# Block-sparse attention and a two-layer network: the first half in another order, and gathers spread over the period

## The chip, the cores and the metric

The kernel runs on one core of a Trainium2 chip. The metric is the device time in microseconds (us) of one execution. A kernel is run several times, and medians are given with the lowest and highest run. Most executions of one kernel agree within about 1%. Each profiled execution gives a span, which is some 1.7 to 2.0 us shorter than the time of the same run. All ledgers below are in terms of the span.

## The reference, cut to what matters

The first part is attention over 4 batches, 8 heads, 768 positions of 64 values, with positions in 24 blocks of 32. A query block sees its two neighbours, itself, the first and the last block, and three blocks drawn at random per query block (`sampled_blocks`). The first and the last query block see everything.

```python
scores = scale * np.matmul(q, k.transpose(0, 1, 3, 2))
mask = np.abs(blk_i - blk_j) <= 1                    # neighbours
mask = mask | (blk_i == 0) | (blk_j == 0) | (blk_i == 23) | (blk_j == 23)
for qb in range(24):
    for kb in sampled_blocks[qb]:                    # three drawn blocks
        mask[qb*32:(qb+1)*32, kb*32:(kb+1)*32] = True
attn = softmax(where(mask, scores, -1e9))
x = matmul(attn, v)                                  # -> (3072, 512)
h = x @ w_in                                         # (512, 2048)
out = gelu_exact(h) @ w_out                          # (2048, 512)
```

## The kernel before

The kernel goes through eight halves: 4 batches times 2 halves of 384 positions. Each half has an attention part (for four pairs of heads: scores `s`, exponentials `pt`, weighted sums `og`), transposes of the result (`psx`, copied into `xT`), a first layer (`hp`, 64 matmuls of 128x384 and 8 Gelus into `g`) and a second layer (`op`). TensorE does the matmuls, ScalarE (ACT) the exponentials and Gelus, VectorE (DVE) most copies and sums, GpSimd (POOL) the gathers, SyncE (SP) issues most DMAs. From the second half on, the second layer of one half is interleaved with the attention of the next. In the first half there is nothing to interleave.

The drawn blocks are gathered on the chip: GpSimd copies key columns (`kg`) and value rows (`v_gat`) by index. V is stored in bf16 (`v_flat`) together with three copies of itself rotated by 32, 64 and 96 partitions, so that each drawn block is also found in the partitions where the kernel uses it. DMAs from `v_flat` to `v_flat` make the rotated copies. So the gather of V depends on this chain: V lands, V is cast, three rotated copies land, three gathers per half run.

The setup and the first half, cut:

```python
st_pool = ...; p_pool = ...
first = first_ctx.enter_context(tc.tile_pool(name="first", bufs=1))   # setup tiles
...
def load_v(b):
    t = stv_pool.tile([P, NT, H, D], F32, tag="st_v", name="st_v")
    for n in range(NT):                                   # six DMAs, 256 KB each
        sp.dma_start(out=t[:, n], in_=v[b, :, n*P:n*P+P].rearrange("h p d -> p h d"))
...
pool.tensor_sub(ok, smp, qbt)           # index arithmetic of V on GpSimd, 15 operations
...
def rotate_v(b, r):
    for lo, hi, src in ((0, P - 32*r, 32*r), (P - 32*r, P, 0)):
        sp.dma_start(out=v_all[lo:hi, NT*r:NT*r+NT], in_=v_own[b % 2][src:src+hi-lo])
...
for hp in range(NPAIR):                                   # four pairs of heads
    ...  # cast and transpose q and k of this pair
    gather_k(0, 0, hp, st)
    if hp == 0:
        load_w_in(0); value_columns(); value_indices(0, dve); mark_valid(0); clear_rest()
    elif hp == 1:
        load_w_in(1)
        own_v(0, first_v, 0, dve); own_v(0, first_v, 1, act)     # casts of V
        for r in range(1, 4):
            rotate_v(0, r)
for s in range(4):
    global_v(0, s, dve)
for c in range(len(VCH)):
    gather_v(0, 0, c)
for c in range(2, 4):
    load_w_in(c)
mark_valid(1)
value_indices(1, pool)                                    # indices for odd batches
first_ctx.close()
x_pool = ctx.enter_context(tc.tile_pool(name="x_pool", bufs=2))   # takes over that memory
...
weave(attention_steps(0, 0, st), [])    # per pair: scores, then the weighted sums of the pair before
for c in range(4):
    load_w_out(c)
load_batch(1)                           # V of batch 1 on SyncE, keys and queries on GpSimd
```

`normalise` takes its scratch tile `rc` from `x_pool`. `x_pool` reuses the memory of the setup tiles.

The first layer of a half, and what is put between its steps:

```python
def step(m):                                              # eight of these
    hp_ = sc_pool.tile([P, 2, 512], F32, tag="sc", name="hp")   # two buffers
    for i in range(2):
        for ki in range(KIN):
            pe.matmul(hp_[:, i, 0:HALF], lhsT=w_in_sb[...], rhs=xT[:, ki, :], ...)
    act.activation(g[:, m:m + 2, :], hp_[:, :, 0:HALF], AF.Gelu)
...
for half in range(2 * B):
    if hb == 0:
        aux = v_steps(b, 1) + k_steps(b, 1, range(NPAIR))       # gathers for the next half
        if b > 0 and more: aux += t_steps(b + 1, (0, 1))        # q, k of the next batch
    elif b == 0: ...
    elif more:
        aux = k_steps(b + 1, 0, (0, 1)) + v_steps(b + 1, 0) + ...
    for step in spread(hidden_steps(b, hb, sts[b]), aux): step()
    ...
    weave(attention_steps(next half), output_steps(this half))
```

The softmax here doesn't subtract the row's maximum and nothing guards it: scores larger than these inputs give would overflow.

Of the kernel before, what the change touches and what calls it, by code (L numbers as in the profile page):

```python
# [10 lines left out]
F32 = mybir.dt.float32  # L11
# [68 lines left out]
def kernel(  # L80
# [24 lines left out]
    p_pool = ctx.enter_context(tc.tile_pool(name="p_pool", bufs=2))  # L105
    first_ctx = ExitStack()
# [15 lines left out]
    def load_v(b):  # L122

        t = stv_pool.tile([P, NT, H, D], F32, tag="st_v", name="st_v")
        for n in range(NT):
            sp.dma_start(out=t[:, n], in_=v[b, :, n * P:n * P + P].rearrange("h p d -> p h d"))
        return t
# [10 lines left out]
    src = dataclasses.replace(sampled_blocks.tensor, shape=[NB, NR * 2], dtype=I32)  # L138
    sp.dma_start(out=raw, in_=bass.AP(tensor=src, offset=0, ap=[[0, P], [1, NB * NR * 2]]))

    first_st = {}
    for hp in range(NPAIR):
        first_st["k", hp] = load_first("k", hp, sp)
        first_st["q", hp] = load_first("q", hp, sp)
        if hp == 1:
            first_v = load_v(0)

    def iota(out, pattern, base, mult):
# [10 lines left out]
                       pattern=[[-1, P]], channel_multiplier=1)  # L159
    lane = msk.tile([P, 1], F32, name="lane")  # L160
# [26 lines left out]

    sbi = msk.tile([P, NB, NR], I32, name="sbi")
# [26 lines left out]
    part8 = msk.tile([P, 2], I32, name="part8")  # L215
    dve.tensor_single_scalar(part8[:, 0:1], part_i, 7, op=ALU.bitwise_and)
    dve.tensor_single_scalar(part8[:, 1:2], part_i, 8, op=ALU.bitwise_and)
    lane8 = msk.tile([P, 2], F32, name="lane8")
    dve.tensor_copy(lane8, part8)
    pool.tensor_scalar(lane8[:, 0:1], lane8[:, 0:1], float(GW), None, op0=ALU.mult)  # L220
    pool.tensor_scalar(lane8[:, 1:2], lane8[:, 1:2], 0.125, None, op0=ALU.mult)
    slotm = msk.tile([P, NR], F32, name="slotm")
    for s in range(NR):
        pool.tensor_scalar(slotm[:, s:s + 1], slot, float(s), None, op0=ALU.is_equal)

# [3 lines left out]
    dve.tensor_tensor(turn, smp_i, slot_i.unsqueeze(2).to_broadcast([P, NQ, NR]), op=ALU.subtract)  # L229
    dve.tensor_single_scalar(turn, turn, 3, op=ALU.bitwise_and)  # L230
    colf = msk.tile([P, NQ, NR], F32, name="colf")
    dve.tensor_copy(colf, turn)
    dve.tensor_single_scalar(turn, smp_i, 2, op=ALU.arith_shift_right)
    rowf = msk.tile([P, NQ, NR], F32, name="rowf")
    dve.tensor_copy(rowf, turn)
    dve.scalar_tensor_tensor(colf, colf, 6.0, rowf, op0=ALU.mult, op1=ALU.add)
    dve.tensor_scalar(colf, colf, -float(NULL), None, op0=ALU.add)


    ok = msk.tile([P, NQ, NR], F32, name="ok")  # L240
    pool.tensor_sub(ok, smp, qbt)
    pool.tensor_mul(ok, ok, ok)
    pool.tensor_scalar(ok, ok, 3.5, None, op0=ALU.is_gt)
    glob = msk.tile([P, NQ, NR], F32, name="glob")
    pool.tensor_scalar(glob, smp, -1.0, float(NB - 1), op0=ALU.mult, op1=ALU.add)
    pool.tensor_mul(glob, glob, smp)
    pool.tensor_scalar(glob, glob, 0.5, None, op0=ALU.is_gt)
    pool.tensor_mul(ok, ok, glob)
    differ = msk.tile([P, NR, NQ], F32, name="differ")
    pairs = ((1, 0), (2, 0), (2, 1))  # L250
    for n, (a, c) in enumerate(pairs):
        pool.tensor_sub(differ[:, n], smp[:, :, a], smp[:, :, c])
    pool.tensor_mul(differ, differ, differ)
    pool.tensor_scalar(differ, differ, 0.5, None, op0=ALU.is_gt)
    for n, (a, c) in enumerate(pairs):
        pool.tensor_mul(ok[:, :, a], ok[:, :, a], differ[:, n])

    def value_columns():
        dve.tensor_mul(colf, colf, ok)
        for s in range(NR):  # L260
            dve.scalar_tensor_tensor(
                base_v, colf[:, :, s], slotm[:, s:s + 1], base_v, op0=ALU.mult, op1=ALU.add)
        dve.tensor_scalar(valid, base_v, float(NULL) - 0.5, None, op0=ALU.is_lt)
# [20 lines left out]

    mask_x = const.tile([P, NT, P], BF16, name="mask_x")
    kgl = [[const.tile([P, P], BF16, name=f"kgl{i}{hp}") for hp in range(NPAIR)] for i in range(2)]
    qgl = [const.tile([P, P], BF16, name=f"qgl{hp}") for hp in range(NPAIR)]
    vgl = [const.tile([P, NPAIR, 2 * VW], BF16, name=f"vgl{i}") for i in range(2)]
    n_all = (NAT1 + NT) * H * GW
    v_flat = const.tile([P, 2 * -(-n_all // DW) * DW], BF16, name="v_flat")  # L290
    v_all = v_flat[:, 0:2 * n_all].rearrange("p (n h e) -> p n h e", h=H, e=2 * GW)
    v_gat = [const.tile([P, NQH, H, 2 * GW], BF16, name=f"v_gat{i}") for i in range(2)]
    v_own = [v_all[:, 0:NT], v_all[:, NAT1:NAT1 + NT]]
    for t in kgl[0] + qgl:
        dve.memset(t, 0.0)

    def clear_rest():
        dve.memset(v_flat[:, 2 * NULL * H * GW:], 0.0)
        for i in range(2):
            dve.memset(v_own[i][:, :, :, D:2 * GW], 1.0)  # L300
# [6 lines left out]
        for i in range(2):  # L307
            dve.memset(vgl[i], 0.0)
            for h in range(2):
                dve.memset(vgl[i][64 * h:64 * h + 64, :, h * VW + D:h * VW + D + 1], 1.0)  # L310
        for t in kgl[1]:
            dve.memset(t, 0.0)
# [11 lines left out]
    def load_w_in(c):  # L324
        pool.dma_start(out=w_in_sb[:, :, 512 * c:512 * c + 512],
                            in_=w_in_v[:, :, 512 * c:512 * c + 512])

    def load_w_out(c):
        pool.dma_start(out=w_out_sb[:, 4 * c:4 * c + 4, :], in_=w_out_v[:, 4 * c:4 * c + 4, :])
# [3 lines left out]
    def own_v(b, st_v, i, eng):  # L333
        n = slice(3 * i, 3 * i + 3)
        cast(eng, v_own[b % 2][:, n, :, 0:D], st_v[:, n])

    def rotate_v(b, r):

        for lo, hi, src in ((0, P - 32 * r, 32 * r), (P - 32 * r, P, 0)):
            sp.dma_start(out=v_all[lo:hi, NT * r:NT * r + NT],  # L340
# [11 lines left out]
    def gather_v(b, hb, c):  # L352
# [3 lines left out]
            v_flat.bitcast(F32).rearrange("p (n e) -> p n e", e=DW),  # L356
# [20 lines left out]
    def gather_k(b, hb, hp, st):  # L377
        kg = kg_pool.tile([P, NQH, P], BF16, tag="kg", name="kg")
# [7 lines left out]
    def scores(b, hb, hp, st):  # L386
# [3 lines left out]
        pt = p_pool.tile([P, 2, 2, 512], BF16, tag="pt", name="pt")  # L390
# [165 lines left out]
    sts = [dict() for _ in range(B)]  # L556
    st = sts[0]
    first_bf = {}
    for hp in range(NPAIR):
        for w in "kq":  # L560
            t = first.tile([P, 2, NT * D], BF16, name=f"bf_{w}{hp}")
            act.copy(t, first_st[w, hp])
            transpose_qk(0, hp, w, t, dve if w == "k" else act, st)
            globals_qk(0, hp, w, dve, st)
        gather_k(0, 0, hp, st)
        if hp == 0:
            load_w_in(0)
            value_columns()
            value_indices(0, dve)
            mark_valid(0)  # L570
            clear_rest()
        elif hp == 1:
            load_w_in(1)
            own_v(0, first_v, 0, dve)
            own_v(0, first_v, 1, act)
            for r in range(1, 4):
# [123 lines left out]
```

## Time and profile before

The three runs before the prediction gave a median of 349.69 us (347.67 to 350.56). The profiled execution took 350.82 us, a little above that range, and has a span of 349.0 us.

| what | before |
|---|---|
| V cast, rotated copies issued | 27.2 us |
| first gather of V starts, last one ends | 47.4, 55.5 us |
| first matmul of the first layer (first hp) | 74.9 us |
| first-layer stage of the first half, first hp to next scores | 11.6 us |
| first hp of batch 1 | 148.9 us |
| span | 349.0 us |

The table of stretches of the kernel before gives, for each stretch of time, its length, the busy time of each engine with the number of instructions, the granted TensorE clock as a share of full speed, the DMA share and GB/s.

```profile
core 0: us, PE busy (x) PEld busy (x) DVE busy (x) ACT busy (x) POOL busy (x), PEclk, DMA share, GB/s
0.00:75.00 75.00, 25.12 (x409) 19.76 (x410) 34.05 (x125) 22.71 (x30) 32.88 (x68) 1.00 0.87 176
75.00:149.00 74.00, 64.49 (x883) 39.34 (x893) 29.22 (x61) 37.26 (x49) 25.94 (x34) 0.98 0.58 114
149.00:349.00 200.00, 175.92 (x2243) 106.25 (x2267) 71.34 (x147) 94.86 (x126) 56.62 (x69) 0.99 0.27 67
```

In the first 75 us TensorE is busy a third of the time, and no other engine is busy for half of it. The prediction reads such a stretch as a chain of dependencies. The DMA share of 0.87 leaves a rival reading, that the stretch is limited by the bytes it moves. After the stretch, TensorE is busy for 88% of the time.

The timeline of the kernel before shows that chain. The columns are start, duration, engine, operation, what it writes and reads, and in brackets the idle time of the engine ahead of it with what ended it. SPq and ACTq lines are issues of DMAs by a sequencer, not the transfers.

```profile
3.16 9.57 SPq L54 DMA_DIRECT2D st_v<-in_v_dram  x6
...
26.07 1.04 DVE L54 CAST v_flat<-st_v 128x1536 bf16<-128x1536 f32 x1
27.19 6.47 SPq L54 DMA_DIRECT2D v_flat<-v_flat  x6
33.70 14.23 SPq L54 DMA_DIRECT2D st_v<-in_v_dram  x6
...
47.41 1.66 POOL L54 INDIRECT_COPY v_gat_222<-v_flat,idx_v_163 128x1024 f32 x1 [10.47 <-DMA st_v<-in_v_dram]
51.06 1.66 POOL L54 INDIRECT_COPY v_gat_222<-v_flat,idx_v_163 128x1024 f32 x1 [2.00 <-issue]
54.03 1.45 POOL L54 INDIRECT_COPY v_gat_222<-v_flat,idx_v_163 128x768 f32 x1 [1.31 <-issue]
...
60.92 0.17 DVE L54 RECIPROCAL rc<-od 128x2 f32<-128x2 f32 x1 [17.54 <-POOL idx_v_164 L54]
...
74.14 0.73 DVE L54 COPY xT<-xdT 128x128 bf16<-128x128 bf16 x1
74.93 2.76 PE L54 MATMUL hp<-xT,w_in_sb 128*128 128x384 bf16 x16 [1.27 <-DVE xT L54]
78.63 7.96 PE L54 MATMUL hp<-xT,w_in_sb 128*128 128x384 bf16 x48 [0.94 <-ACT g L54]
86.52 0.34 PE L54 MATMUL s_983<-tq,tk 64*128 64x128 bf16 x6
```

The reader is to see four things. The cast of V ends at 27, and the copies are issued at once. The first gather names a load of V as its releaser, but it reads `v_flat`; the loads of the next V were issued in the same stretch, and the profile names the event that came last. The first two gathers start 3.65 us apart although each is busy for 1.66. VectorE waits 17.5 us, to 60.9, for GpSimd's last write of an index tile that `rc` has nothing to do with: this is the reuse of memory.

How much of that wait reaches TensorE is told by TensorE's own list of waits, here of the first 75 us of the kernel before (total, number of times, longest):

```profile
PE og L54 <- POOL v_gat_222 L54: 11.6, 3, 5.6
...
PE od L54 <- DVE xd L54: 3.0, 1, 3.0
```

TensorE lost 3.0 us behind the tile that VectorE's wait delayed, not 17.5. Most of VectorE's wait lay beside TensorE's own waits for the gathers. The same list from 149 us on, the steady part, holds these:

```profile
PE psx L54 <- DVE xT L54: 4.7, 5, 1.9
...
PE ps L54 <- DVE tk L54: 1.6, 2, 0.8
...
PE ps L54 <- DVE tq L54: 0.7, 2, 0.3
```

### The profile page before, as it was taken

The numbers are of one execution on the slowest core, as the hardware profiler recorded it, in microseconds if no ns is written. First come the engines' busy times: TensorE is split into PE (matmuls) and PEld (weight loads), VectorE is DVE, ScalarE is ACT, GpSimd is POOL, SyncE is SP. The second block draws the span as 40 slices with busy tenths as digits, with TensorE's granted clock in tenths as the row PEclk, the third lists the DMA queues.
The fourth block names the chain that finished last, engine by engine and source line by source line (L and its number), as shares of the span: only waits on it lengthen the run. The fifth ranks groups of instructions, "written<-read, shape, count | busy, mean of one in ns | idle before, by whom it ended". The sixth has DMA issues, their size and how long they took to land. (4 is left out here: it accounts for less than half of the span.)

```text
span 349.0 us, 8094 instructions
## 1 busy us (share of the span) xinstructions
PE 265.5 (76%) x3532; PEld 165.3 (47%) x3568; DVE 134.6 (39%) x333; ACT 154.8 (44%) x205; POOL 115.4 (33%) x171
## 2 busy tenths in 40 slices
PE   1216103779889878897879989888989898989995
PEld 1115002655555545454545565454645564555552
DVE  6785200530454614714641438233634343025101
ACT  3427103326653365344633576146524771664420
POOL 3603137744101455434313545332215453200000
PEclk9999999999999989999998999999999999999999
DMA  6967975995099401910297349000750001001001
GB/s 215 240 156 164 206 152 78 187 201 81 2 251 234 69 2 34 198 43 2 68 254 160 73 67 178 32 2 2 211 162 2 3 32 62 2 27 37 30 31 61
DMA packets 43252, 34.98 MB, mean 100 GB/s; under 512 B 26192, under 2 KB 38608, under 8 KB 43216
## 3 DMA queue, kind: packets, MB, share of 16 engines
q1 hardware_dynamic: 32656, 25.54, 29.0%
q0 software_dynamic: 10560, 8.91, 16.8%
q8 instruction: 28, 0.46, 0.5%
q14 instruction: 8, 0.07, 0.1%
HBM read 27.34 MB, written 6.29 MB: 96 GB/s over the span
## 5 line engine op out<-in xcount | busy, mean ns | idle before, releaser
L54 PE MATMUL op<-w_out_sb,g 128*128 128x512 bf16 x348 | 88.7, 387 | 4.6 <-issue 4.0
L54 ACT ACTIVATE g<-hp 128x768 bf16<-128x768 f32 x64 | 51.8, 811 | 89.9 <-PE hp L54 89.9
L54 PE MATMUL hp<-xT,w_in_sb 128*128 128x384 bf16 x512 | 86.8, 327 | 2.2 <-DVE xT L54 1.3
L54 POOL INDIRECT_COPY kg<-tk,idx_k 128x704 f32 x32 | 40.6, 1268 | 81.1 <-issue 44.4
L54 PEld LDWEIGHTS <-w_in_sb 128*128 128x128 bf16 x512 | 49.5, 98 | 36.4 <-issue 3.4
L54 DVE TENSOR_TENSOR pt<-pt,mask_x 128x768 bf16<-128x768 bf16 x32 | 22.9, 718 | 90.3 <-ACT pt L54 90.3
L54 PEld LDWEIGHTS <-g 128*128 128x128 bf16 x384 | 34.5, 99 | 33.6 <-issue 2.2
L54 PEld LDWEIGHTS <-pt 128*32 128x32 bf16 (+1 forms) x992 | 24.1, 100 | 23.4 <-issue 19.9
L54 DVE COPY tk<-ps 128x768 bf16<-128x768 bf16 x16 | 15.2, 947 | 40.5 <-PE ps L54 40.5
L54 ACT ACT_TABLE_LOAD x16 | 20.5, 1283 | 15.4 <-PE hp L54 7.0
L54 ACT ACTIVATE pd<-sd 128x768 bf16<-128x768 f32 x16 | 13.0, 813 | 31.0 <-PE sd L54 30.8
L54 DVE COPY os<-op 128x512 f32<-128x512 f32 x24 | 16.5, 686 | 23.4 <-PE op L54 23.4
L54 POOL INDIRECT_COPY v_gat_222<-v_flat,idx_v_164 128x1024 f32 (+1 forms) x6 | 9.5, 1587 | 41.6 <-DMA st_v<-in_v_dram 20.6
L54 PEld LDWEIGHTS <-tk 64*128 64x128 bf16 (+1 forms) x288 | 13.8, 102 | 20.1 <-issue 17.4
L54 PEld LDWEIGHTS <-kg 64*128 64x128 bf16 x704 | 13.2, 94 | 13.1 <-issue 8.8
L54 POOL INDIRECT_COPY v_gat_222<-v_flat,idx_v_163 128x1024 f32 (+1 forms) x6 | 9.5, 1586 | 28.4 <-issue 17.9
L54 DVE TENSOR_TENSOR x<-og,rc 128x384 bf16<-128x384 f32 x32 | 17.8, 557 | 1.1
L54 PE MATMUL psx<-ident,x 128*128 128x128 bf16 x96 | 9.8, 226 | 8.7 <-DVE xT L54 5.8
L54 PE MATMUL og<-v_gat_222,pt 128*32 128x65 bf16 x352 | 6.8, 207 | 11.6 <-POOL v_gat_222 L54 11.6
L54 PEld LDWEIGHTS <-x 128*128 128x128 bf16 x96 | 7.0, 101 | 14.2 <-issue 9.2
L54 POOL INDIRECT_COPY v_gat_223<-v_flat,idx_v_163 128x1024 f32 (+1 forms) x6 | 9.5, 1575 | 11.5 <-issue 9.2
L54 DVE COPY xT<-psx 128x512 bf16<-128x512 bf16 (+1 forms) x24 | 9.6, 402 | 9.4 <-PE psx L54 9.2
(360 smaller groups left out, 321.2 us busy)
## 6 DMA issues: line engine op xcount, KB each, us to landing
st_v<-in_v_dram SPq DMA_DIRECT2D x24, 256.0 KB, 5.1
out_dram<-os SPq DMA_DIRECT2D x24, 256.0 KB, 2.6
v_flat<-v_flat SPq DMA_DIRECT2D x8, 594.0 KB, 6.1
v_flat<-v_flat SPq DMA_DIRECT2D x8, 396.0 KB, 6.7
st<-in_k_dram POOLq DMA_DIRECT2D x6, 384.0 KB, 8.8
st<-in_q_dram POOLq DMA_DIRECT2D x6, 384.0 KB, 10.2
w_in_sb<-in_moe_w_in_dram POOLq DMA_DIRECT2D x4, 512.0 KB, 7.6
w_out_sb<-in_moe_w_out_dram POOLq DMA_DIRECT2D x4, 512.0 KB, 9.2
```

The costliest lines, as they stand in the source:

```text
L54: return self._tc.keep_in_program_order(f(*args, **kwargs))
```

## The change

The intent is to shorten the chain of the first half and to spread GpSimd's work. V is loaded ahead of the other pairs and cast tile by tile, and the rotated copies are issued right after. The index arithmetic moves from GpSimd to VectorE. The scores of all four pairs run while the copies and gathers of V are under way, and the four weighted sums follow together. `x_pool` is allocated first, so its tiles reuse no setup memory. Keys and queries of the later three pairs are loaded by GpSimd straight into bf16, which saves six of ScalarE's eight casts (0.83 us each). The weights come in four DMAs of 1 MB where there were eight of 512 KB. V of batch 1 is issued from ScalarE's queue inside the first Gelu stage. From the second half on, gathers move out of the Gelu stages into the attention parts too, and one VectorE step copies four pieces where four separate steps did.

The diff, cut to its core:

```diff
+    x_pool = ctx.enter_context(tc.tile_pool(name="x_pool", bufs=2))
     first_ctx = ExitStack()
-    def load_v(b):
+    def load_v(b, eng):
...
-            sp.dma_start(out=t[:, n], in_=v[b, :, ...])
+            eng.dma_start(out=t[:, n], in_=v[b, :, ...])
...                              # ok, differ, glob: 15 pool operations removed
     def value_columns():
-        dve.tensor_mul(colf, colf, ok)
+        dve.tensor_sub(ok, smp, qbt)
+        dve.tensor_mul(ok, ok, ok)
+        ...                      # 14 more, all on VectorE, then base_v as before
...
     def load_w_in(c):
-        pool.dma_start(out=w_in_sb[:, :, 512*c:512*c+512], ...)
+        f = slice(1024 * c, 1024 * c + 1024)
+        pool.dma_start(out=w_in_sb[:, :, f], in_=w_in_v[:, :, f])
...
+    first_pair(0); clear_mask(); clear_globals(0, dve); first_pair(1)
+    for n in range(NT):
+        own_v(0, first_v, n, n + 1, (dve, act)[n % 2])
+    for r in (2, 1, 3):
+        rotate_v(0, r, sp)
+    value_columns(); value_indices(0, dve)
+    scores(0, 0, 0, st); dense_scores(0, st)
+    for c in range(2):
+        load_w_in(c)
+    first_pair(2); scores(0, 0, 1, st); first_pair(3)
+    ...                          # scores of pairs 2 and 3, gather_v, global_v
+    value_indices(1, dve)
+    for c in range(2):
+        load_w_out(c)
+    dense_weighted(0, 3, st); transpose_xd(st)
+    for hp in range(NPAIR):
+        weighted(0, 0, hp, st)
+    for m in range(MH):
+        transpose_x(0, 0, m, st)
+    place_xd(0, 0, st)           # the last copy into xT
-    weave(attention_steps(0, 0, st), [])
...
-        if hb == 0:
-            aux = v_steps(b, 1) + k_steps(b, 1, range(NPAIR))
...
+        for n, step in enumerate(spread(hidden_steps(b, hb, sts[b]), aux)):
+            step()
+            if half == 0 and n == 0:
+                sts[1]["st", "v"] = load_v(1, act)
+        if half == 0:
+            load_batch(1)
...
+            after[0] = own_steps(b + 1)
+            if b > 0:
+                after[3] = k_steps(b + 1, 1, (0,))
+                after[4] = k_steps(b + 1, 1, (1,))
+                after[len(main) - 4] = v_steps(b + 1, 0)
```

## The prediction

> **What bounds the kernel now.** In the table of stretches TensorE is busy 25.1 of the first 75.0 us and 240.4 of the remaining 274 (88%). TensorE's timeline has the first hidden-layer matmul (hp) at 74.93 us; afterwards its waits sum to roughly 28 us, half of it short turns that must stay. So the first 75 us are a dependency chain, the rest is TensorE.
>
> **The chain of the first 75 us (timelines, waits).** V has landed at 16.5 us, but VectorE, held by a wait for GpSimd's index arithmetic, the indices and 6.5 us of memsets, casts its half only at 26.1; the rotated copies of V are issued from 27.2 and in place at about 45. The three gathers of V end at 55.5 (3.65 us each with their gaps). VectorE waits 17.5 us, to 60.9, for GpSimd's last index write: the normalisation's scratch reuses the memory of the setup tiles. Only then do the remaining pairs run.
>
> **What changes.** V is cast tile by tile as it lands; rotated copies start near 17 us, beside the first weights. From the traffic of before (copies, one weight chunk and the next V took about 18 us together) I estimate that the copies, sharing with 4.2 MB of weights, are in place near 38. Index arithmetic moves to VectorE (some 30 operations of 0.2 to 0.4 us, 8.4 us), after the copies' issue. Scores of all four pairs fit in before 38. Gathers of V: 38 + 3 x 3.65 = 49. Then four weighted sums and the transposes, about 7 us: first hp at 56.5 instead of 74.9. Gain 18.4 us. The reuse wait vanishes: that scratch is now allocated earlier.
>
> **What it costs.** V of batch 1 is issued from ScalarE's queue, after the first of eight Gelus. Six such issues took 5.6 us on SyncE with little beside them, 9.6 and 14.2 in traffic (SyncE's timeline), holding the sequencer. [...] this trace says about 1 us each. hp has two buffers, so TensorE stalls in the first hidden stage: I estimate 7 us (5 to 11). The second-layer weights, issued near 50, land before that stage ends.
>
> **Later.** GpSimd starts earlier in each stage: waits for kg (3.7 us in batch 1's first half), for xT behind a VectorE copy of rotated V (about 2.5 us), and doubled transposes waiting for VectorE (2.3 us) should mostly go: minus 5 us. Larger weight DMAs save nothing by themselves.
>
> 349.7 - 18.4 + 7 - 5 = 333; I predict **332 us**, 80% range **321 to 343**. Faster by over 2%: 0.91; within 2%: 0.07; slower: 0.02.
>
> **What would show it.** First hp near 56 us (52 to 61); rotated copies issued near 17; v_gat done near 49; no VectorE wait on an index tile. In the first hidden stage a gap of 5 to 11 us between first and second Gelu, filled by DMA issues, and a TensorE wait for g nearly as long; that stage's end near 75 instead of 86.5. TensorE busy within 5 us. Later stages equal or up to 3 us shorter per batch.
>
> **What would make it wrong.** If issues on ScalarE don't hold it, the end is near 325. If the weights slow the rotated copies further, or VectorE's index arithmetic delays the later pairs' keys so that the gathers of V start late, first hp comes at 62 or later and the gain shrinks to 12 us. If batch 1's keys and queries, now loaded after the first hidden stage, arrive late, TensorE stalls near 95 us.

349.7 - 18.4 + 7 - 5 came to 333, and the 7 us are an estimate from the issue times of 5.6 to 14.2 us in the trace of before.

## The result, and the profile after

The changed kernel took 333.77 us (median of 4 runs, 333.33 to 336.02) against 349.74 us (347.67 to 350.56, 4 runs). The ratio is 0.9565, with a 95% interval of 0.9505 to 0.9625. Here and below, a ratio is the mean time of one kernel's fast runs over the mean time of the other's in the same rounds, so it is not quite the ratio of the medians that are quoted.

The profiled spans are 349.0 and 332.2 us. They differ by 16.8 us and the medians by 16.0, since the profiled run of before was slower than its median. The ledger, read from TensorE's timelines:

| | before | after | difference | predicted |
|---|---|---|---|---|
| rotated copies issued | 27.2 | 21.5 | | near 17 |
| first gather of V starts | 47.4 | 43.5 | | 38 |
| last gather of V ends | 55.5 | 51.6 | | 49 |
| first hp | 74.9 | 60.6 | -14.3 | 56.5 (-18.4) |
| first-layer stage of the first half | 11.6 | 18.5 | +6.9 | +7 |
| from there to the end | 262.5 | 253.1 | -9.4 | -5 |
| span | 349.0 | 332.2 | -16.8 | -16.4 |

The stretches of the changed kernel, cut at the first hp, at the end of that stage and at the first hp of batch 1:

```profile
0.00:60.60 60.60, 23.70 (x408) 18.98 (x409) 36.89 (x142) 18.35 (x26) 23.01 (x37) 0.98 0.84 155
60.60:79.10 18.50, 14.64 (x65) 7.36 (x65) 0.46 (x6) 6.84 (x8) 9.05 (x9) 0.79 0.76 137
79.10:139.20 60.10, 52.60 (x819) 32.65 (x829) 29.05 (x61) 30.29 (x41) 20.25 (x30) 1.00 0.73 142
139.20:332.20 193.00, 173.67 (x2243) 105.38 (x2267) 69.78 (x147) 94.81 (x126) 55.50 (x69) 1.00 0.28 69
```

TensorE's work in the first half is nearly the same, 23.7 us against 25.1; the stretch became shorter because less of it is waiting. The second stretch has a granted clock of 0.79 where the others have about 1.

The timeline of the changed kernel, with the lines that answer to those of before:

```profile
2.22 15.07 SPq L54 DMA_DIRECT2D st_v<-in_v_dram  x6
20.85 0.62 ACT L54 CAST v_flat<-st_v 128x512 bf16<-128x512 f32 x1 [1.49 <-DMA st_v<-in_v_dram]
21.49 5.37 SPq L54 DMA_DIRECT2D v_flat<-v_flat  x6
43.51 1.66 POOL L54 INDIRECT_COPY v_gat<-v_flat,idx_v 128x1024 f32 x1 [7.36 <-issue]
50.12 1.44 POOL L54 INDIRECT_COPY v_gat<-v_flat,idx_v 128x768 f32 x1 [1.30 <-issue]
...
57.77 2.79 DVE L54 COPY xT<-xdT 128x128 bf16<-128x128 bf16 x1
58.86 1.64 POOL L54 INDIRECT_COPY v_gat<-v_flat,idx_v 128x1024 f32 x1 [2.01 <-issue]
60.61 6.40 PE L54 MATMUL hp<-xT,w_in_sb 128*128 128x384 bf16 x24 [3.22 <-DVE vgl L54]
63.54 3.21 ACTq L54 DMA_DIRECT2D st_v<-in_v_dram  x3
64.69 0.81 ACT L54 ACTIVATE g<-hp 128x768 bf16<-128x768 f32 x1
66.79 3.13 ACTq L54 DMA_DIRECT2D st_v<-in_v_dram  x3
69.97 1.51 ACT L54 ACTIVATE g<-hp 128x768 bf16<-128x768 f32 x2 [4.47 <-issue]
70.83 8.34 PE L54 MATMUL hp<-xT,w_in_sb 128*128 128x384 bf16 x40 [3.82 <-ACT g L54]
79.10 0.34 PE L54 MATMUL s<-tq,tk 64*128 64x128 bf16 x6
```

Three readings follow. First, SyncE's sequencer needed 15.07 us to issue the six loads of the first V, where before it needed 9.57. Other loads of keys and queries ran at the same time. The last tile of V was cast at 21.5, not at 17. That the slow issue is the reason is not shown: in e5 below the issue took 10.85 us, and the last cast still ended at 21.6. Second, the last VectorE copy into `xT` took 2.79 us. It took 0.73 before, and such a copy is a matter of 0.3 us (it took 0.18 to 0.44 in the seven later halves of the changed kernel, and ScalarE did the same copy in 0.30 us in an experiment below). Third, ScalarE issued the six loads of V between its first Gelus. The gap between the first and the second is 4.47 us, the stretch of issues is filled, and TensorE waited 3.82 us for `g`.

The matmuls of that stage also took longer each. The 24 ones from 60.61 took 6.40 us, 0.27 us each; before, the 48 ones from 78.63 took 7.96 us, 0.17 us each. The records of the granted clock, read in stretches of 2 us, give 0.50 from 60.6 to 65.0, 1.00 to 70.8, a mean of 0.73 to 73, 0.50 to 75, and nearly 1 from there. TensorE idled 3.22 us ahead of the first hp and 3.82 us inside the stage, and its matmuls then ran at the recorded 0.50 for 4.4 us and for about 3.4 us (worked out from the means). Read in stretches of 0.5 us, the clock is at 0.50 from 58.5 on, about 1 us after TensorE had gone idle, and again from 72.0 on, about 1 us after its work had resumed. What makes the clock fall and come back is not shown: in e1 below, TensorE idled 4.70 us ahead of the first hp, and the record gives 1.00 from 57.0 to 70.0.

So the +6.9 us of this stage consist of about 2.9 us more waiting (3.82 against 0.94) and 4.0 us of slower matmuls (14.74 us of `hp` against 10.72).

TensorE's waits from the first hp of batch 1 to the end of the changed kernel, those answering to the three lines shown of before:

```profile
PE psx L54 <- DVE xT L54: 2.4, 5, 0.5
```

The waits for `xT` fell from 4.7 to 2.4 us, and those for `tk` and `tq` (2.3 us) are gone from the list. In the part between, waits for `kg` fell from 3.7 to 1.2 us. These are the later gains.

### The profile page after: what moved, and what is told of

It is laid out like the page before. It is cut to its first block, busy times and chain, and to the rows that moved or that the text cites. A ratio compares the mean times of both kernels' runs of the same rounds, so it can differ in the third digit from the quotient of the medians.

```text
span 332.2 us, 8067 instructions
## 1 busy us (share of the span) xinstructions
PE 264.6 (80%) x3532; PEld 164.4 (49%) x3568; DVE 136.2 (41%) x356; ACT 150.3 (45%) x201; POOL 107.8 (32%) x144
## 3 DMA queue, kind: packets, MB, share of 16 engines
q0 software_dynamic: 11072, 10.09, 20.1%
## 5 line engine op out<-in xcount | busy, mean ns | idle before, releaser
L54 PE MATMUL hp<-xT,w_in_sb 128*128 128x384 bf16 x512 | 90.7, 336 | 7.1 <-ACT g L54 3.8
L54 PE MATMUL op<-w_out_sb,g 128*128 128x512 bf16 x348 | 86.2, 379 | 4.4 <-issue 3.8
L54 ACT ACTIVATE pt<-s 128x1024 bf16<-128x1024 f32 (+2 forms) x96 | 58.9, 687 | 27.2 <-issue 11.6
L54 POOL INDIRECT_COPY kg<-tk,idx_k 128x704 f32 x32 | 39.3, 1229 | 84.4 <-issue 66.8
L54 POOL INDIRECT_COPY v_gat<-v_flat,idx_v 128x1024 f32 (+1 forms) x24 | 38.2, 1591 | 79.2 <-issue 44.4
L54 DVE TENSOR_TENSOR pt<-pt,mask_x 128x768 bf16<-128x768 bf16 x32 | 20.1, 630 | 103.8 <-ACT pt L54 103.6
L54 ACT ACT_TABLE_LOAD x16 | 20.5, 1283 | 30.7 <-PE hp L54 24.1
L54 DVE COPY tk<-ps 128x768 bf16<-128x768 bf16 x16 | 15.3, 956 | 27.3 <-PE ps L54 27.2
L54 DVE COPY os<-op 128x512 f32<-128x512 f32 x24 | 16.5, 687 | 23.7 <-PE op L54 23.7
L54 PE MATMUL ps<-ident,st 128*64 128x128 bf16 x384 | 16.7, 244 | 11.7 <-ACT st L54 9.2
L54 PEld LDWEIGHTS <-st 128*64 128x64 bf16 x384 | 13.5, 124 | 16.4 <-ACT st L54 9.4
L54 PE MATMUL s<-tq,kg 64*128 64x32 bf16 x704 | 14.2, 175 | 8.6 <-ACT g L54 4.4
L54 PE MATMUL sd<-qgl,tk 128*128 128x128 bf16 x96 | 9.2, 240 | 13.6 <-ACT pt L54 13.6
L54 PE MATMUL og<-v_gat,pt 128*32 128x65 bf16 x704 | 12.4, 199 | 7.0 <-POOL v_gat L54 7.0
## 6 DMA issues: line engine op xcount, KB each, us to landing
w_in_sb<-in_moe_w_in_dram POOLq DMA_DIRECT2D x2, 1024.0 KB, 20.6
```

The costliest lines, as they stand in the source:

```text
L54: return self._tc.keep_in_program_order(f(*args, **kwargs))
```

## The experiments

The theory after the result, which the experiments then had to test: the total came from the order of the first half and the order of the loop. The order gave 14 us, of which a few were lost to VectorE being held beside the gathers, and half was given back to issues of V on ScalarE. The rivals: the gain came from the vanished reuse wait (17.5 us in VectorE's list), from larger weight DMAs, or from taking the index arithmetic off GpSimd. All experiments change the kernel after, except one that changes the kernel before. Every result was correct. The runs were made on three chips; each was compared with the kernel before on its own chip, whose medians there were 350.82 (group of e1 to e4), 351.17 (e5 to e8) and 351.77 us (e9 to e12).

| run | median (range, runs) us | ratio to before (95%) | first hp | stage | first hp of batch 1 | span |
|---|---|---|---|---|---|---|
| before | 349.74 (347.67-350.56, 4) | 1 | 74.9 | 11.6 | 148.9 | 349.0 |
| after | 333.77 (333.33-336.02, 4) | 0.9565 (0.9505-0.9625) | 60.6 | 18.5 | 139.2 | 332.2 |
| e1 | 333.08 (329.1-334.76, 6) | 0.9464 (0.9401-0.9527) | 61.3 | 12.8 | 138.2 | 331.0 |
| e2 | 333.91 (331.84-335.59, 6) | 0.9521 (0.9469-0.9573) | 58.3 | 12.8 | 136.8 | 331.0 |
| e3 | 333.86 (331.88-335.64, 6) | 0.9506 (0.9453-0.956) | 56.2 | 21.8 | 138.0 | 332.2 |
| e4 | 339.22 (337.48-339.63, 4) | 0.965 (0.9589-0.9711) | 67.2 | 17.5 | 144.7 | 337.8 |
| e5 | 332.74 (331.51-335.8, 6) | 0.946 (0.9418-0.9501) | 60.0 | 19.7 | 139.8 | 334.0 |
| e6 | 332.02 (331.31-332.59, 4) | 0.945 (0.9408-0.9492) | 60.2 | 15.8 | 136.0 | 330.8 |
| e7 | 341.77 (340.82-342.03, 4) | 0.9725 (0.9683-0.9768) | 59.7 | 19.6 | 142.1 | 340.0 |
| e8 | 325.54 (324.13-326.99, 6) | 0.9269 (0.9233-0.9305) | 57.9 | 12.8 | 130.0 | 324.4 |
| e9 | 348.41 (345.01-350.41, 4) | 0.9946 (0.9879-1.0012) | 71.4 | 12.2 | 145.8 | 343.2 |
| e10 | 335.47 (334.68-336.09, 4) | 0.955 (0.9491-0.961) | 58.5 | 20.1 | 139.1 | 334.1 |
| e11 | 336.88 (336.63-338.36, 4) | 0.9608 (0.9545-0.967) | 60.2 | 20.7 | 141.0 | 335.3 |
| e12 | 322.31 (321.33-327.16, 6) | 0.9171 (0.9122-0.922) | 54.2 | 13.0 | 127.7 | 322.0 |

One run each of e1 (334.76), e9 (350.41) and e12 (327.16) fell in the slow state; they are in the medians and ranges but not in the ratios. All profiled runs are fast ones. The first hp of the kernels e5, e7 and e10, whose first half is that of after or nearly so, scatters between 58.5 and 60.6. Their first-layer stage scatters as well (18.5 to 20.1 us, with after). Differences of 2 us in those columns are not worth an explanation unless the timeline shows their cause.

One caution holds for every comparison with after. It was not run again beside the experiments, and medians and ratios disagree about them. By medians e1, e2, e3, e5 and e6 lie within 1.8 us of after. By ratios (their difference times 351 us) they lie 3.5, 1.5, 2.1, 3.7 and 4.0 us below it, and only the intervals of e5 and e6 are clear of after's. So whether these five gained such amounts in total is not settled; what follows rests on the timelines.

### e4: the old order inside the new first half

```diff
-    scores(0, 0, 0, st); dense_scores(0, st)
     for c in range(2): load_w_in(c)
-    first_pair(2); scores(0, 0, 1, st); first_pair(3)
-    ...                                   # scores of all pairs, then weighted sums
+    first_pair(2); first_pair(3); mark_valid(0)
+    for c in range(len(VCH)): gather_v(0, 0, c)
+    for s in range(4): global_v(0, s, dve)
+    value_indices(1, dve)
+    for c in range(2): load_w_out(c)
+    weave(attention_steps(0, 0, st), [])  # pair by pair, as before
```

> The changed kernel, with only the order of the first half put back: scores and weighted sums of the pairs alternate as in the kernel before, so the weighted sum of pair 0 stands in TensorE's queue before the scores of pairs 2 and 3. Theory: after the last gather of V (51.6 us) three pairs of scores must still be done; the kernel before took 19.4 us from its last gather to first hp, the changed kernel 9.0. Expect first hp at 68 to 71 instead of 60.6, total 342 (340 to 345). Rival: the gain comes from V being ready earlier and the order hardly matters: total within 3 us of 333.8.

Measured: 339.22 us, first hp at 67.2, which is 6.6 us later than after although its gathers ended 2.4 us earlier (49.2). By medians and by spans the order is worth 5.5 us, by the ratios 3 us (0.965 against 0.9565, in intervals that overlap). So the direction stands, and the order by itself is worth less than the expected 8 us. From the end of its last gather to the first hp e4 took 18.0 us; before took 19.5 and after 9.0. One line of e4's timeline shows one reason why the old order is dear beside the gathers:

```profile
53.21 4.43 DVE L54 TENSOR_TENSOR pt<-pt,mask_x 128x768 bf16<-128x768 bf16 x1 [2.73 <-ACT pt L54]
```

The multiplication by the mask takes 0.56 us elsewhere. It fell among the gathers for the next half and took 4.43 us. In the new order these multiplications are done before the gathers start.

### e9: the kernel before, with the reuse wait taken away

```diff
 for s in range(4):
     global_v(0, s, dve)
+value_indices(1, pool)
 for c in range(len(VCH)):
     gather_v(0, 0, c)
 ...
 mark_valid(1)
-value_indices(1, pool)
```

The wait is not removed by hand; the index tile is only finished before the gathers.

> The kernel before, with one line moved: the second index computation of GpSimd stands ahead of its gathers of V instead of behind them, where GpSimd is idle anyway. Theory: the wait of 17.5 us that VectorE showed for that index (to 60.9 us) overlaps with the wait for the gathers, which end at 55.5, so only some 4 us of it were on the path. Expect no VectorE wait on an index tile, first hp at 70 to 72.5 instead of 74.9, total 346 to 348 against 350 to 351 for the kernel before. Rival: the wait was the bottleneck of the first half, as its length suggests; then first hp comes 10 us or more earlier and the total is under 341.

Measured: 348.41 us, ratio 0.9946 (0.9879 to 1.0012), so the total is not clearly different. The first hp came at 71.4, 3.5 us earlier, and that of batch 1 3.1 us earlier. (The profiled run was the fastest of e9, so its span of 343.2 flatters it.) VectorE's reciprocal now waits 12.29 us, for TensorE. Of the 3.5 us, 1.4 came from gathers that ran earlier in this run (the last ended at 54.0, not 55.5). From there to the first hp e9 took 17.4 us, against 19.5 before, although its last copy into `xT` took 1.76 us beside a gather (0.73 before). So the wait of 17.5 us was worth some 2 to 3 us, in keeping with the 3.0 us that TensorE's own list showed. The rival "the reuse wait made the gain" falls.

### e10: small weight DMAs

```diff
-        f = slice(1024 * c, 1024 * c + 1024)
+        f = slice(512 * c, 512 * c + 512)
...
-    for c in range(2):
+    for c in range(4):
         load_w_in(c)
```

The second-layer weights were split in the same way.

> The changed kernel, with both weights loaded in four DMAs each as in the kernel before instead of two. Theory: larger weight DMAs save nothing by themselves; GpSimd needs 1.5 us more to issue each weight, and the transfers are limited by the shared DMA engines. Expect total within 1.5 us of the changed kernel's 333.8, weights landing at the same time within 2 us. Rival: the larger rows make the transfers faster, so smaller ones slow the rotated copies and the first gather comes 2 us later or more: total 336 or more.

Measured: 335.47 us, ratio 0.955 (0.9491 to 0.961) against 0.9565. The median is 1.7 us above after's, just outside the expected 1.5; the ratio is not above it, and the first gather of V came at 42.6 (43.5 in after), so not later. GpSimd needed 3.04 us to issue the four first-layer DMAs (1.56 for two in after), and they landed 19.4 us after their issue (20.6 in after, medians). The DMA engines were busy meanwhile (share 1.02 from 21.5 to 43.5 us in after). No effect of the size of the weight DMAs is seen, as the prediction said.

### e11: the index arithmetic back on GpSimd

```diff
+    pool.tensor_sub(ok, smp, qbt)
+    pool.tensor_mul(ok, ok, ok)
+    ...                          # the 15 operations of before
     def value_columns():
-        dve.tensor_sub(ok, smp, qbt)
-        ...                      # nine VectorE operations
```

> The changed kernel, with the index arithmetic (which sampled blocks count) put back on GpSimd, at the place it had before. Theory: its place matters only because in the kernel before it stood between VectorE and the cast of V; here V is cast first, so GpSimd's 5 us of small operations only delay the loads of keys and queries of heads 4 to 7 (to 12 us) and the first key gather (to 17 us), and the rotated copies still end at 41. Expect first gather of V at 40.5 to 43.5 us, total within 2 us of 333.8. Rival: the arithmetic on GpSimd holds the chain again, first gather at 45 or later, total 336 or more.

Measured: 336.88 us, ratio 0.9608 (0.9545 to 0.967), which overlaps with after's interval. Both expectations were missed: the first gather of V came at 44.8 (40.5 to 43.5 expected), and the median is 3.1 us above after's (2 expected), past the 336 that the rival named. VectorE finished the first indices at 24.1 instead of 26.8, since it had fewer of the operations; the first gather of V began 1.3 us later than in after, and the first hp came at the same time; and ScalarE's V issues happened to take 1.7 us longer, which lengthened the stage to 20.7 us. By medians the engine of the arithmetic is worth 3.1 us, by ratios 1.5 us, and these runs do not separate that from zero. So this rival is not shown to give any of the gain.

### e7: the old loop after the new first half

The loop from the second half on was put back, with `load_v` on SyncE in its old place; the first half stayed.

```diff
-        elif hb == 0 and more:
-            for hp in (0, 1):
-                aux += t_steps(b + 1, (hp,)) + k_steps(b + 1, 0, (hp,))
-        ...
-        after[0] = v_steps(nb_, 1) + k_steps(nb_, 1, range(2 * (b > 0), NPAIR))
+        elif hb == 0:
+            aux = v_steps(b, 1) + k_steps(b, 1, range(NPAIR))
+            if b > 0 and more: aux += t_steps(b + 1, (0, 1))
+        ...
```

> The changed kernel's first half, but the order of gathers, casts and copies of V from the second half on as in the kernel before. From the first hp of batch 1 to the end the kernel before took 200.1 us, the changed kernel 193.0. Theory: these 7 us are the spread gathers and the casts moved off VectorE's busy stretches, not the early start. Expect this stretch to take 199 to 201 us again, total 340 (338 to 342). Rival: the stretch was longer in the kernel before through its later start or its clock; then it stays near 193 and the total near 334.

Measured: 341.77 us, span 340.0, which is 7.8 us more than after. From the first hp of batch 1 to the end it took 197.9 us, against 193.0 after and 200.1 before; 199 to 201 were expected. TensorE's waits over that stretch of e7 hold these lines:

```profile
PE psx L54 <- DVE xT L54: 4.9, 5, 1.9
...
PE ps L54 <- DVE tk L54: 1.6, 2, 0.8
...
PE ps L54 <- DVE tq L54: 0.7, 2, 0.3
```

They are the waits of before, to within 0.2 us. They explain 4.8 of the 4.9 us. The other 2.9 us lie before batch 1, where waits for `kg` rose from 1.2 to 3.3 us and those for `xT` from 1.0 to 2.0 (3.1 us together). The loop's order is thus worth 7.8 us by the spans, 8.0 by the medians and 5.6 by the ratios, whose intervals are apart. The 2.2 us between 197.9 and 200.1 have no wait to explain them. They lie within the scatter of the profiles: the stretch took 197.4, 197.9 and 200.1 us in the three kernels with the old loop (e9, e7, before) and 192.8 to 195.0 us in the eleven others. The means differ by 4.4 us, about as much as the waits.

### e1: V of batch 1 on SyncE, behind the first gather

```diff
-            if half == 0 and n == 0:
-                sts[1]["st", "v"] = load_v(1, act)
...
+    fence = const.tile([P, 2], BF16, name="fence")
+    sp.dma_start(out=fence, in_=v_gat[0][:, 0, 0, 0:2])   # waits for the first gather
+    sts[1]["st", "v"] = load_v(1, sp)
```

> The changed kernel, with V of batch 1 issued from SyncE instead of ScalarE; a tiny copy that reads the first gathered V holds it back until then, so that it loads in the stretch (46 to 52 us) in which the DMA engines are idle. Theory: the six issues hold ScalarE between its first and second Gelu (4.5 us gap, TensorE waits 3.8 us for g). Expect: no DMA issue on ScalarE, gap between these Gelus under 1 us, TensorE wait for g about 1 us, total 3 us less (330.5, 329 to 332). Rival: the first hidden stage is long because the clock is lowered there (0.66) and because weights still load; then the total stays at 333 to 334 and the stage's length (18.5 us) hardly changes.

Measured: the first-layer stage fell from 18.5 to 12.8 us, so the issues on ScalarE cost 5.7 us there, clock included. The issues on SyncE took 5.3 us. But the median is 333.08, hardly below 333.77 (by the ratio the gain is 3.5 us, in intervals that overlap), and the first hp of batch 1 came only 1.1 us earlier. Two things took the gain. TensorE waited 4.7 us for `kg` ahead of batch 1 (1.2 in after), since the rotated copies of batch 1 and its gathers of V kept their places in the program (e8 moves both): the gathers of V began at 100.4 us (101.5 in after), and the key gathers came behind them. And the last copy was held still longer, as the timeline of e1 shows:

```profile
56.95 4.27 DVE L54 COPY xT<-xdT 128x128 bf16<-128x128 bf16 x1
57.54 1.64 POOL L54 INDIRECT_COPY v_gat<-v_flat,idx_v 128x1024 f32 x1 [2.01 <-issue]
61.21 1.65 POOL L54 INDIRECT_COPY v_gat<-v_flat,idx_v 128x1024 f32 x1 [2.02 <-issue]
61.28 12.90 PE L54 MATMUL hp<-xT,w_in_sb 128*128 128x384 bf16 x64 [4.70 <-DVE vgl L54]
```

The copy ended at 61.22, just when the next gather began. In after it ended at 60.56, with the end of a gather at 60.50; in e2 and e6, where it took 2.29 and 2.11 us, it ended within 0.1 us of the end of a gather as well. So VectorE was held: these copies lasted until a gather was over, or until the next one started. What decides which of the two goes first is not shown: each of the four copies began in the 2 us ahead of a gather in which GpSimd records no work (in after at 57.77, with gathers that ended at 56.84 and began at 58.86). Nor is the end a rule: the multiplication of e4 ended at 57.64, 1.2 us into a gather. Not every operation was held: `x<-og,rc`, which reads what TensorE wrote, kept its 0.56 us beside a gather (after, at 55.71). That its length, 2.1 to 4.3 us, depends on where among the gathers the copy happens to fall is my reading of four such cases. The stage's 12.8 us are still 1.2 more than before: the matmuls of its start took 0.30 us each (9 in 2.70 us), the pace that goes with a clock of 0.50 in after (8 in 2.39 us from 60.6), with no ScalarE issue in sight (the record of the clock says 1.00 there). The stages of e2, e8 and e12, also without these issues, took 12.8 to 13.0 us. What slows this part is not shown; in e4, with the old order, the first 16 matmuls took 4.38 us too (2.76 in before).

### e2: V of batch 1 on SyncE, without the fence

```diff
-                sts[1]["st", "v"] = load_v(1, act)
+                sts[1]["st", "v"] = load_v(1, sp)
```

> The changed kernel, with V of batch 1 issued from SyncE right behind the rotated copies (about 27 us), nothing holding it back. Theory of issue cost: ScalarE's gap goes as in e1. Theory of contention: 1.6 MB more in the queue while rotated copies and first weights load; the rotated copies, ahead in the same queue, keep their time (first gather still at about 43.5 us, within 1.5), the first weights land by 50, before they are needed: total as e1, 330.5. Rival: the early V takes DMA time from the rotated copies, the first gather comes at 46 or later, and the total is 333 or more.

Measured: 333.91 us, so the expected 330.5 was missed. SyncE issued the loads from 28.1 to 47.4, 19.3 us for six, right in the traffic of the rotated copies and the weights. The first gather of V was not delayed (41.2). The first hp of the second half came 6.8 us earlier than in after, that of batch 1 only 2.5 us: TensorE waited 5.2 us for `kg`. As in e1, the local gain was taken by the same later wait.

e2 also bears on the rival that bytes limit the first half. Ahead of the first hp, before moved about 13.2 MB, after 9.4 and e2 11.0 (estimates, from GB/s times length). e2 moved 1.6 MB more than after, and its first hp came 2.4 us earlier, so these bytes did not set it. What the other traffic is worth that after moved out of the first half was not tested.

### e3: the last copy on ScalarE

```diff
-        dve.tensor_copy(st["xT", hb][:, :, c], st["xdT"][...])
+        cast(eng, st["xT", hb][:, :, c], st["xdT"][...])     # eng = act for half 0
```

> The changed kernel, with the last copy before the first hidden stage (xT from xdT, 128x128, 2.79 us on VectorE) put on ScalarE, which is idle there. Theory: VectorE's copy is held for the length of GpSimd's running gather, which a copy on ScalarE would not be. Expect the copy at 0.2 to 0.4 us, first hp 2 to 2.5 us earlier (58 to 58.7), total 331.5 (330 to 333). Rival: the copy waits for something else that takes until 60.5, such as its input or the weights; then first hp stays at 60.6 and the total at 333.8.

Measured: 333.86 us, no gain in the median (2.1 us by the ratio, in intervals that overlap), but what the edit did is plain in the timeline of e3:

```profile
45.23 0.30 ACT L54 COPY xT<-xdT 128x128 bf16<-128x128 bf16 x1 [6.11 <-DVE xdT L54]
...
56.18 5.85 PE L54 MATMUL hp<-xT,w_in_sb 128*128 128x384 bf16 x24 [0.61 <-DVE xT L54]
59.87 8.16 ACTq L54 DMA_DIRECT2D st_v<-in_v_dram  x4
68.94 9.06 PE L54 MATMUL hp<-xT,w_in_sb 128*128 128x384 bf16 x40 [6.91 <-ACT g L54]
```

The copy took 0.30 us, beside a gather (45.10 to 46.75), and the first hp came at 56.2 instead of 60.6. Of these 4.4 us, 2.1 came from gathers that began earlier in this run (41.45), and the remaining 2.3 are the hold that vanished. That the hold is as long as the gather, as the theory had it, is not what after shows: its copy took 2.79 us and the gather 1.64. Then ScalarE's issues of V took 8.16 us for four (3.13 for the last three in after); that the loads of the second-layer weights, issued from 49.4, slowed them is a guess, not shown. TensorE waited 6.91 us for `g`, and the stage ended at 77.9, 1.2 us earlier than after. A gain ahead of a stage of DMA issues was given back in it.

### e5: keys and queries of the later pairs loaded after the first pair

```diff
     new_x(0, 0, st)
+    first_pair(0)
     for w in "kq":
         st["st", w, 1] = load_qk(0, w, 1)
-    first_pair(0)
```

> The changed kernel, with the loads of keys and queries of heads 4 to 7 issued on GpSimd after its first key gather (about 12 us) instead of at 6.9. Theory: V lands 4 us later than in the kernel before (last cast ends 21.5 instead of 17 to 18) because these 1.6 MB of loads take DMA time from it. Expect the last cast of V to end at 18 to 19.5, rotated copies issued from there, first gather of V at 39 to 41 instead of 41.1 to 43.5, and almost no gain in the end of the first hidden stage, as the V of batch 1 on ScalarE sets that: total 333 (331 to 335). Rival: V lands late because SyncE issues slowly on its own account; then the last cast still ends at 21 or later.

Measured: the last cast of V still ended at 21.6 us. SyncE's issue became shorter (10.85 us), but the moved loads, issued at about 12.5, ran beside the last tiles of V. The first gather came at 42.9 (43.5 in after). The rival, that SyncE issues slowly on its own account, does not fit either: the issue was 4.2 us shorter, and the cast ended no earlier. This is a miss: the edit did not give V the free way that it was meant to give, so what an earlier V would be worth stays open.

### e6: first-layer weights after the key gathers

```diff
     scores(0, 0, 0, st); dense_scores(0, st)
-    for c in range(2): load_w_in(c)
     first_pair(2); scores(0, 0, 1, st); first_pair(3)
+    for c in range(2): load_w_in(c)
```

> The changed kernel, with the first weights issued on GpSimd only after the key gathers of all four pairs (about 35.6 us instead of 21.7). Theory: the rotated copies took 20 us because the weights share the DMA engines; alone they should take about 10 us from 21.5 and be in place at 32 to 33, so GpSimd's own queue sets the first gather of V: 39.5 to 40.5 us. The weights then land near 51, before first hp at 57 to 58.5. Total 333 (331 to 335), as in e3. Rival: the rotated copies are slow by themselves and first gather stays at 41 to 43.5.

Measured: 332.02 us. The rotated copies landed in 5 to 8 us where they needed 7 to 14 in after (medians of the three pairs, from issue to landing), and the first gather of V came at 39.3, 4.2 us earlier than in after. So the weights did hold the copies, and the copies the weights: these landed in 10.2 us instead of 20.6. But the first hp moved by only 0.5 us. The timeline of e6 shows the new obstacle:

```profile
41.15 2.19 DVE L54 TENSOR_SCALAR own<-base_v 128x22 f32<-128x22 f32 x1
43.37 1.84 DVE L54 TENSOR_TENSOR base_v<-base_v,own 128x22 f32<-128x22 f32 x1
...
45.34 2.13 DVE L54 COPY idx_vf<-base_v 128x6 f32<-128x6 f32 x1
...
50.55 0.29 DVE L54 TENSOR_TENSOR xd<-od,rc 128x128 bf16<-128x128 f32 x1
```

The second index computation, operations of 0.16 to 0.26 us in after, now fell beside the gathers and took up to 2.19 us each. It pushed `xd`, which the transposes need, from 42.8 to 50.6. Here the same hold hit tiny operations.

### e8: three repairs together

e8 takes the fence of e1, the ScalarE copy of e3, and in addition issues the rotated copies of batch 1 ahead of that batch's keys and queries, with its first gathers of V right after the second half's first scores:

```diff
         if half == 0:
+            for f in own_steps(1):       # casts and rotated copies of batch 1
+                f()
             load_batch(1)
...
-            after[0] = own_steps(b + 1)
+            after[0] = own_steps(b + 1) if b > 0 else v_steps(1, 0)
```

> The changed kernel with e1 (V of batch 1 from SyncE in the idle stretch), e3 (last copy on ScalarE), and the rotated copies of batch 1's V issued before that batch's keys and queries are loaded (about 68 us instead of 87), with its gathers of V following at once. Theory: e1 and e3 won 4 to 8 us by the second hidden stage and lost most of it again, because the gathers of batch 1's V started at 100 us whatever came before, held by rotated copies that shared the DMA engines with the keys and queries. Expect V gathers of batch 1 from 80 to 86 us, waits of TensorE for kg under 1.5 us in batch 1, first hp of batch 1 at 131 to 133 instead of 139.2, total 326 (324 to 329). Rival: keys and queries of batch 1, now behind the rotated copies, land later and hold the transposes: first hp of batch 1 at 137 or later, total 332 or more.

Measured: 325.54 us, as expected. The gathers of V for batch 1 began at 84.7 instead of 101.5, the wait for `kg` (4.7 us in e1) is gone from TensorE's list ahead of batch 1, and the first hp of batch 1 came at 130.0. In after, the DMA share was 1.33 from 80 to 87 us, with batch 1's keys and queries on their way, and the rotated copies, issued from 85.5 on, landed in 4.1 to 8.7 us. The first gather of V for batch 1, in after and then in e8:

```profile
101.50 1.65 POOL L54 INDIRECT_COPY v_gat<-v_flat,idx_v 128x1024 f32 x1 [21.83 <-DVE vgl L54]
...
84.74 1.65 POOL L54 INDIRECT_COPY v_gat<-v_flat,idx_v 128x1024 f32 x1 [2.82 <-DVE pt L54]
```

What e1 and e3 gained locally now reaches the end, because the next limit was moved in the same edit.

### e12: with e6 and an earlier index computation

e12 is e8 with the weights of e6, and with the second index computation moved ahead of the gathers:

```diff
     dense_weighted(0, 0, st)
+    value_indices(1, dve)
     mark_valid(0)
...
-    value_indices(1, dve)
     for c in range(2):
         load_w_out(c)
```

> e8, with the first weights issued after the key gathers (as in e6) and the second index computation done by VectorE before the gathers of V start. Theory: in e6 the gathers of V ended 3.5 us earlier (47.5), but VectorE's small index operations, now beside running gathers, took 1.8 to 2.1 us each instead of 0.2, and TensorE's queue waited 10.8 us for the value behind them. Expect index operations at 0.2 us again, gathers of V over at 47.5, first hp at 53.5 to 55, total 322 (320.5 to 324). Rival: the weights, issued at 35, are now late for first hp, or the early index operations delay the scores of pairs 2 and 3: first hp at 57 or later, total 325.5 as in e8.

Measured: 322.31 us, ratio 0.9171. The index operations took 0.17 to 0.28 us each at 32 to 35 us, the gathers of V began at 39.2, and the first hp came at 54.2:

```profile
54.21 13.06 PE L54 MATMUL hp<-xT,w_in_sb 128*128 128x384 bf16 x64 [0.61 <-DVE xT L54]
```

Set beside e6, this shows that the hold of the index operations was what had kept e6's gain from the first hp. e12 is the fastest version, 11.5 us below the changed kernel by medians.

## Why the prediction was right or wrong

The total was right: 332 us predicted, 333.77 measured. Its three terms were -18.4, +7 and -5 us; measured were -14.3, +6.9 and -9.4. Two errors of 4 us cancelled, so that the total came this close is luck.

**The chain of the first half, -18.4 predicted, -14.3 measured.** The mechanism held: V earlier, copies earlier, scores ahead of the gathers, weighted sums after. The term was mis-sized in two steps. "Rotated copies start near 17 us" was 21.5, because the last tile of V landed at about 21. Why it did is open: the issue of V took 15.1 us of SyncE's sequencer, but with 10.85 us in e5 the tile was no earlier. "In place near 38" was about 41.5 (the first gather's start at 43.5 less the 2 us that precede each gather); the duration of the copies, 20 us, was as estimated. That is 3.5 us. The gathers then took slightly less than 11 us and ended at 51.6. From there to the first hp the prediction allowed 7.5 us, and it took 9.0: the last copy, at 2.79 us in place of some 0.3, is the cause, and e3 shows that without it 2.3 us go. The prediction had counted the weights' traffic into "near 38"; e6 shows what it costs: with the weights later, the gathers start 4.2 us earlier.

Of the 14.3 us, 3.9 lie ahead of the end of the last gather (55.5 to 51.6) and 10.4 behind it (19.5 to 9.0 us). The 10.4 are the order: with the old order put back, e4 takes 18.0 us there. No run takes the 3.9 us apart.

**The index tile.** VectorE's wait on it is gone, as predicted. What it was worth the prediction did not say apart; e9 shows some 2 to 3 us, in the kernel before.

**ScalarE's issues of V, +7 predicted, +6.9 measured.** The gap between the first two Gelus was filled by DMA issues, as predicted, but at 4.47 us it was just below the range of 5 to 11. TensorE's wait was 3.82 us, 2.9 more than before. The rest, 4.0 us, was lowered clock, which the prediction did not name: right size, partly wrong reason. e1 splits it: without the issues the stage takes 12.8 us, so 5.7 us belong to the issues with the clock drop around their gap, and 1.2 us to slow matmuls at the start, whose cause stays open. A single load of V took a median of 1.08 us to issue on SyncE in after, but six in a row held a sequencer for 5.3 us at least (e1) and 19.3 us at most (e2).

**Later gains, -5 predicted, -9.4 measured.** The waits named were the right ones: `kg` 3.7 to 1.2 us, `xT` 4.7 to 2.4, `tk` and `tq` 2.3 to none, together 7.1 us; the prediction counted on only a part. The remaining 2.3 us are lower busy time of TensorE for the same 2243 matmuls from batch 1 on (175.92 to 173.67 us). No edit explains them, and they lie within the scatter given under e7: before's 200.1 us is the longest of its three stretches, and after's 193.0 near the shortest of its eleven. So the term was too small by about 2 us, and the rest is chance. e7 shows that the loop's order makes these waits: put back, it costs 7.8 us by the spans. The expectation that stages would become "up to 3 us shorter per batch" held.

**Larger weight DMAs save nothing; TensorE busy within 5 us.** Both held (e10; 265.5 and 264.6 us).

What stays open: how early V could be cast with nothing beside its loads (e5 failed to arrange that), whether the index arithmetic's engine is worth a few us (e11), and what the bf16 loads of keys and queries and the traffic moved out of the first half are worth, which no run isolates.

## What to carry to other kernels

A long wait in the list of a side engine says little; read what the limiting engine lost behind it (here 3.0 us of 17.5). VectorE operations beside GpSimd gathers were held here for up to 4.43 us (e4), small index operations of 0.2 us for up to 2.19 (e6); put ahead of the gathers these took 0.17 to 0.28 us (e12), and a copy on ScalarE took 0.30 (e3). Here local gains (e1 333.08 us, e3 333.86) reached the end only when the next arrival, the rotated copies and key gathers of the next batch, was moved up as well (e8 325.54), so repairs have to be tried together before one of them is dismissed.

## Times of single operations, as measured

- One load of V, of 1024 pieces of 256 bytes, took a median of 1.08 us to issue on SyncE in after (0.43 to 5.59, 18 loads), and loads of V landed a median of 5.4 us after their issue (3.4 to 13.8). Six of them held the issuing sequencer for 5.3 us (e1), 9.6 us (before), 15.1 us (after) and 19.3 us (e2); on ScalarE such issues delayed Gelus (a gap of 4.47 us in after). A load of one pair's keys in longer pieces took 0.45 us to issue (after).
- A GpSimd gather of 128x704 takes 1.2 us in the records of after, with the next one starting 3.27 us after, and one of 128x1024 takes 1.65 us with the next one 3.65 us after. The 2 us between are shown as idle, but in e1 a VectorE copy stayed held through them (56.95 to 61.22).
- The VectorE operations held beside a gather that are shown took 1.8 to 4.4 us in place of 0.16 to 0.56 us.
- The recorded clock of TensorE was 0.50 in after for 4.4 and about 3.4 us of work. It fell about 1 us after TensorE went idle, or after it had resumed. In e1 the records gave 1.00 while nine matmuls took 0.30 us each, the pace at a recorded 0.50 in after; durations are the safer reading.
